# Delta-rule attention with a hard-swish MLP on one core: first steps reordered, runs of small matmuls joined in pairs

## The chip, the cores and the metric

The kernel runs on one core of a Trainium2 chip. The metric is the device time of one execution in microseconds (us), as the median of several. A profiled execution also gives a span, from its first to its last instruction, which is 2 us or so shorter. Ratios are the mean time of one kernel's runs over that of the kernel before in the same rounds on the same chip, so they are not quite the ratio of the medians that stand beside them. In the profile's lines PE is TensorE (PEld its weight loads), DVE is VectorE, ACT ScalarE, POOL GpSimd and SP SyncE; SPq and ACTq are the issuing of DMA transfers by SyncE and ScalarE.

## The reference

```python
# attention: q, k, v of (4, 8, 768, 48), beta of (4, 8, 768)
k_n = k / (np.linalg.norm(k, axis=-1, keepdims=True) + 1e-06)
for t in range(S):
    y[:, :, t] = np.einsum('bhd,bhde->bhe', q[:, :, t], state)
    v_old = np.einsum('bhde,bhd->bhe', state, kt)
    state = state + bt[:, :, :, None] * np.einsum('bhd,bhe->bhde', kt, vt - v_old)
# bridge to x of (3072, 384), then the MLP with w_in (384, 2048), w_out (2048, 384)
h = x @ w_in
g = h * np.clip(h + 3.0, 0.0, 6.0) / 6.0
out = g @ w_out
```

The weights arrive as 64-bit floats, so the kernel has to make 32-bit floats of them on the chip.

## The kernel before

The sequence is cut into 24 steps of 32 tokens, four steps to a group. What has to be told apart in the traces:

- **Norms** of a group's keys (a square, a reduction, a Newton iteration on VectorE).
- **Preparation** of one step: normalized keys kb and masks mb on GpSimd, eight transposes (pt) on TensorE, 64 small score matmuls (sc), the masked scores LB on VectorE, half of which go to DRAM.
- **Substitution** for a group: it reads the scores back as A, then does 30 pairs of VectorE operations (pr, A), and writes the result through DRAM into LB.
- **Chain** of one step: ks (state times keys), R = v - ks, pz (LB times R), Z, py (state times queries plus LB times Z), y, its transposes (yt, the "seam"), su (the state's update). Each of ks, pz, su, sc and the two halves of py is a run of 64 matmuls on 32x32 to 64x64 pieces of the array.
- **MLP units**: `up` makes one 128-column block of h (ph, 6 matmuls), ScalarE's t and VectorE's gate g; `down` is four matmuls into po.
- **Conversion** of one weight tile: five VectorE operations and one on ScalarE. Eight tiles make w_in, eight w_out; `need(n)` places conversions until n tiles are done.

The instructions of each engine stand in the order in which this Python text emits them, so the schedule is the order of the `take` calls:

```python
    def take(gen, n=1):                # emit the next n parts of a generator
        for _ in range(n):
            next(gen, None)
    ...
        for t in range(GS):            # GS = 4; queries, keys and weights all on SyncE
            load_k(GS + t)
        drain(norms(0, 0, 1))
    ...
        take(conv, 2)
        drain(norms(1, 0, GS))         # second norms, then the first substitution
        inv = inverse(0, nc.scalar)
    ...
        for t in range(CB):            # CB = 2
            load_v(t + 2)
            for _ in chain(t):
                take(conv, 2)          # two conversion operations per part of a chain
    ...
        for t in range(CB, N):         # the main loop: one step of the chain, 16 MLP units
            g, i = divmod(t, GS)
            load_v(t + 2)
            ...
            elif i == 2 and t + GS // 2 < N:
                fill = inverse(g + 1, nc.sync)
                for n in range(GS):
                    load_k((g + 2) * GS + n)
            ...
            for u in range(NU // 2 if early else NU):     # early: steps 2 and 3, 8 units each
                if i < 2 and preps:
                    at(u, preps[2 * i : 2 * i + 2])
                if early or u % 2 == 0:
                    take(ch)
                if early:
                    need(min(NWI, ((t - CB) * NU // 2 + u) // 2 + 1))
                else:
                    take(conv, 2)
                take(units)
                take(fill, 3 if early else 1 + (u % 2 == 0))
```

## Time and profile before

| | before |
|---|---|
| median of the first three runs | 855.86 us (854.84 to 857.21) |
| span of the profiled run | 853.4 us |
| busy: TensorE / VectorE / ScalarE / GpSimd | 82% / 40% / 22% / 9% |
| start of step 2, 4, 6 | 129.4, 193.6, 274.6 us |

The strip of the page cuts the span in 40 slices; a digit is the busy share of TensorE in tenths, and the second line is its granted clock. Before:

```profile
PE   1113248557789979999989999799999999999997
PEclk9966558687899979999989999999999999999999
```

TensorE is full from about the thirteenth slice on (one slice is 21.3 us), with a dip in the fifteenth, the twenty-first and the twenty-sixth; in front of that it is half empty, at a clock that falls to half. How the rest of the profile is read is the first part of the prediction.

### The profile page before, as it was taken

To read this page: it belongs to the slowest core of one execution; us is meant where nothing else is said; L and a number is where in the kernel's file an instruction comes from. 1 tells how busy PE (TensorE), PEld (TensorE's weight loads), DVE (VectorE), ACT (ScalarE), POOL (GpSimd) and SP (SyncE) were. 2 spreads that over 40 slices of the span, in tenths; PEclk is the share of its full clock that TensorE was granted. 3 is DMA by queue.
4 is the path that set the end of the run, shared out by engine and by line. 5 is a ranking of instruction groups with operands and counts; after the bars stand their busy time and mean duration, and the time that the engine had idled before them with its cause. 6 is when DMAs were issued, how large, how long until landed. Compare 5 with 4: busy or idle time off the path is not lost.

```text
span 853.4 us, 24929 instructions
## 1 busy us (share of the span) xinstructions
PE 703.6 (82%) x11208; PEld 507.6 (59%) x11208; DVE 344.5 (40%) x865; ACT 188.5 (22%) x377; POOL 78.8 (9%) x118
## 2 busy tenths in 40 slices
PE   1113248557789979999989999799999999999997
PEld 1112236444557657677567686586776867768684
DVE  5049663865562285022662122850237411212020
ACT  2121122122222014132132141141321312213030
POOL 3213300030210002100002200021000000000000
PEclk9966558687899979999989999999999999999999
DMA  5451573032421402122220214020120300000000
GB/s 114 100 118 29 132 205 73 2 96 77 128 64 41 91 20 60 29 50 49 66 56 19 44 28 95 20 61 18 27 49 19 72 12 20 2 20 2 19 0 19
DMA packets 140138, 45.76 MB, mean 54 GB/s; under 512 B 130272, under 2 KB 133344, under 8 KB 140032
## 3 DMA queue, kind: packets, MB, share of 16 engines
q1 hardware_dynamic: 127200, 41.45, 21.5%
q10 hardware_dynamic: 12832, 2.72, 1.6%
q8 instruction: 88, 1.44, 0.7%
q14 instruction: 18, 0.15, 0.1%
HBM read 33.13 MB, written 11.01 MB: 52 GB/s over the span
## 4 chain that ended last, share of the span: by engine, by line
PE 66%; DVE 11%; issue 8%; DMA 6%; SPq 5%; ACT 2%; POOL 1%; ACTq 0%; POOLq 0%; DVEq 0%
PE ph L469 29%; PE po L490 24%; SPq L86 4%; DVE pr L327 2%; DVE A L331 2%; DMA d<-in_moe_w_out_dram 2%; PE py L379 2%; PE pt L282 2%; PE pz L379 2%; PE su L438 2%; PE sc L295 2%; PE py L369 2%; PE ks L369 1%; DMA A<-l_dram 1%; DMA l_dram<-LB 1%
## 5 line engine op out<-in xcount | busy, mean ns | idle before, releaser
L469 PE MATMUL ph<-xT,w_in 128*128 128x256 f32 x1152 | 289.6, 403 | 17.5 <-DVE w_in L200 9.1
L490 PE MATMUL po<-w_out,g 128*128 128x384 f32 x768 | 272.2, 500 | 4.4 <-DVE w_out L200 4.4
L469 PEld LDWEIGHTS ph<-xT,w_in 128*128 128x128 f32 x1152 | 221.4, 199 | 54.1 <-DVE w_in L200 9.5
L490 PEld LDWEIGHTS po<-w_out,g 128*128 128x128 f32 x768 | 141.6, 193 | 89.3 <-DVE w_out L200 4.5
L478 DVE SCALAR_TENSOR_TENSOR g<-t,ph 128x256 f32<-128x256 f32 x192 | 80.5, 419 | 206.9 <-ACT t L474 206.9
L474 ACT ACTIVATE t<-ph,half 128x256 f32<-128x256 f32 x192 | 90.7, 473 | 224.4 <-PE ph L469 211.7
L327 DVE TENSOR_TENSOR pr<-A 128x30 f32<-128x30 f32 (+9 forms) x180 | 61.6, 342 | 65.8 <-DMA A<-l_dram 61.0
L282 PE MATMUL pt<-ident,kb 128*128 128x128 f32 x96 | 17.6, 314 | 57.7 <-POOL kb L260 57.7
L331 DVE TENSOR_TENSOR A<-A,pr 128x30 f32<-128x30 f32 (+9 forms) x180 | 61.3, 341 | 6.2
L260 POOL TENSOR_TENSOR kb<-kf,inv 128x384 f32<-128x384 f32 x24 | 21.2, 883 | 417.1 <-DVE inv L247 350.3
L282 PEld LDWEIGHTS pt<-ident,kb 128*128 128x128 f32 x96 | 13.1, 160 | 62.0 <-POOL kb L260 58.7
L285 ACT ACTIVATE KQ<-pt 128x512 f32<-128x512 f32 x48 | 28.2, 596 | 82.4 <-PE pt L282 54.4
L446 DVE TENSOR_TENSOR state<-state,su 128x384 f32<-128x384 f32 x46 | 23.3, 548 | 55.8 <-PE su L438 55.8
L301 DVE TENSOR_TENSOR LB<-sc,mb 128x512 f32<-128x512 f32 x24 | 16.4, 685 | 69.2 <-PE sc L295 69.2
L267 POOL TENSOR_TENSOR mb<-beta_tok,mask 128x256 f32<-128x256 f32 x48 | 34.3, 734 | 107.1 <-DVE LB L301 107.1
L496 ACT ACTIVATE o<-po 128x384 f32<-128x384 f32 x24 | 11.8, 492 | 141.7 <-PE po L490 141.7
L295 PE MATMUL sc<-KQ 64*32 64x64 f32 x1536 | 21.9, 242 | 20.8 <-ACT KQ L285 20.8
L379 PE MATMUL pz<-R,LB 32*32 32x48 f32 x1472 | 22.9, 216 | 19.3 <-issue 10.7
L379 PEld LDWEIGHTS pz<-R,LB 32*32 32x32 f32 x1472 | 19.7, 115 | 30.6 <-issue 19.0
L295 PEld LDWEIGHTS sc<-KQ 64*32 64x32 f32 x1536 | 17.9, 114 | 29.6 <-ACT KQ L285 22.9
L168 ACT ACTIVATE e<-e,rebias 128x768 uint32<-128x768 uint32 x16 | 15.0, 935 | 78.8 <-DVE e L165 71.8
L379 PEld LDWEIGHTS py<-Z,LB 32*32 32x32 f32 x1536 | 19.1, 109 | 20.5 <-issue 11.3
(54 smaller groups left out, 384.1 us busy)
## 6 DMA issues: line engine op xcount, KB each, us to landing
d<-in_moe_w_in_dram SPq DMA_DIRECT2D x8, 768.0 KB, 5.3
d<-in_moe_w_out_dram SPq DMA_DIRECT2D x8, 768.0 KB, 4.4
kf<-in_k_dram SPq DMA_DIRECT2D x96, 48.0 KB, 2.2
qb<-in_q_dram SPq DMA_DIRECT2D x96, 48.0 KB, 2.2
vf<-in_v_dram SPq DMA_DIRECT2D x96, 48.0 KB, 2.6
out_dram<-o SPq DMA_DIRECT2D x96, 48.0 KB, 1.6
A<-l_dram SPq DMA_DIRECT2D x5, 512.0 KB, 3.8
x_dram<-A SPq DMA_DIRECT2D x5, 512.0 KB, 3.1
```

Source lines behind the costliest of these rows:

```text
L86: nc.sync.dma_start(out=kfs[g][rows(b), i], in_=tokens(k, b, t))
L267: nc.gpsimd.tensor_tensor(out=mb[:, e], in0=beta_tok[:, t, e:H:2].unsqueeze(2).unsqueeze(3).to_broadcast([P, NP, 2, C]), in1=mask2[:].unsq ...
L282: nc.tensor.transpose(pt[:, p, :], src[:, 2 * p : 2 * p + 2].rearrange("p e w -> p (e w)"), ident[:])
L285: nc.scalar.activation(out=KQ[:, :, j, :], in_=pt[:], func=ACTF.Copy)
L295: nc.tensor.matmul(scv[rows(b), e, p], lhsT=KQ[r, p, 0, rows(b)], rhs=KQ[r, p, :, rows(b)], start=True, stop=True,)
L327: nc.vector.tensor_tensor(out=pv, in0=A[:, j, j + 1 :].unsqueeze(1).to_broadcast([128, j, n]), in1=A[:, 0:j, j].unsqueeze(2).to_broadcast( ...
L331: nc.vector.tensor_tensor(out=A[:, 0:j, j + 1 :], in0=A[:, 0:j, j + 1 :], in1=pv, op=ALU.subtract)
L379: nc.tensor.matmul(place(h, b), lhsT=m(h)[rows(b)], rhs=z[rows(b), D * h : D * h + D], start=start, stop=True, skip_group_check=True, tile ...
L469: nc.tensor.matmul(ph[:], lhsT=w_in[:, s, f * 128 : (f + 1) * 128], rhs=xT[:, s, :], start=(s == 0), stop=(s == NKT - 1),)
L474: nc.scalar.activation(out=t1[:], in_=ph[:], func=ACTF.Relu, bias=half[:, 0:1], scale=1.0 / 6.0)
L478: nc.vector.scalar_tensor_tensor(out=g[:], in0=t1[:], scalar=1.0, in1=ph[:], op0=ALU.min, op1=ALU.mult)
L490: nc.tensor.matmul(po[:], lhsT=gs[blk, f][:, c * P : (c + 1) * P], rhs=w_out[:, f, :], start=(f == 0), stop=(f == NFC - 1),)
```

## The change

The intent: start the MLP sooner, keep the waits of the first 275 us short, and make fewer and longer runs of small matmuls. Core of the diff (cuts marked with dots, the comments added here):

```diff
-    def load_q(t):
+    def load_q(t, eng=nc.sync):
...
     def convert():
-        split_w(0)                 # e of tile i+1 was made before tile i was finished
-        yield
         for i in range(NW):
-            split_w(i + 1)
-            yield
             if i in raws:          # now one tile from its first to its last operation
...
-                load_w(i + 2)      # in the middle of a conversion
...
             done[0] = i + 1
+            if i + 2 not in raws and i + 2 > 4:
+                load_w(i + 2)      # at its end
...
-            nc.scalar.activation(out=sq[:], in_=kf[:, i0 + i], func=ACTF.Square)
+            if g == 0:
+                nc.scalar.activation(out=sq[:], in_=kf[:, i0 + i], func=ACTF.Square)
+            else:
+                nc.gpsimd.tensor_tensor(
+                    out=sq[:], in0=kf[:, i0 + i], in1=kf[:, i0 + i], op=ALU.mult
+                )
...
             R = Rt[:]
+            of_state(py, 1)        # the state half of py directly behind ks
             yield
...
+        with tc.tile_pool(name="early", bufs=3) as early:    # raw tiles of weights 0 to 2
+            for t in range(GS):
+                load_k(t)
+                load_q(t, nc.scalar)
...
+            inv1 = norms(1, 0, GS)                           # second norms between the
+            for t in range(1, GS):                           # first preparations
...
+            need(1)
+            inv = inverse(0, nc.scalar)
+            take(inv)
+            for t in range(GS):                              # preparations 4 to 7 inside
+                take(prep_of(GS + t))                        # the first substitution
+                take(inv, 4)
...
+            need(2)
             for t in range(CB):
                 load_v(t + 2)
                 for _ in chain(t):
-                    take(conv, 2)
+                    take(conv)
+            for n in range(GS):
+                load_k(2 * GS + n)
+            need(3)
...
+            if i == 1 and (g + 2) * GS < N:                  # keys one step earlier
+                for n in range(GS):
+                    load_k((g + 2) * GS + n)
+            if i == 2 and t > CB:
+                drain(fill)
+                fill = chained(norms(g + 2, 0, GS) ..., inverse(g + 1, nc.sync) ...)
...
+            plan = {
+                0: lambda: (take(ch), now and take(now[1])),
+                3: lambda: (take(ch), now and take(now[0])),  # pz, then scores
+                7: lambda: (take(ch), now and take(now[1])),  # py, then scores
...
                 if early:
-                    need(min(NWI, ((t - CB) * NU // 2 + u) // 2 + 1))
+                    need(min(NWI, ((t - CB) * NU + u) // 4 + 1))
```

## The prediction

> **What bounds the kernel now.** I read the granted clock first (0.920 over the span, one core), then the strip of 40 slices, then busy times by stage, then timelines of the stages that lose time. I cut stages where a step's first run of small matmuls starts (ks, the state times the keys): step 2, the first with MLP work, at 129.7 us, step 4 at 193.6, step 6 at 274.6. The busy times by stage (columns: stretch, its length, then busy us and count of PE, PEld, DVE, ACT and POOL, the TensorE clock, the DMA share, GB/s):
>
> ```profile
> 0.00:129.70 129.70, 35.43 (x1102) 29.00 (x1102) 71.81 (x174) 23.89 (x39) 28.31 (x54) 0.72 0.50 115
> 129.70:193.57 63.87, 41.52 (x743) 31.13 (x735) 39.58 (x108) 12.72 (x27) 7.76 (x8) 0.77 0.25 57
> 193.57:274.58 81.01, 66.97 (x1096) 46.11 (x1095) 42.87 (x65) 21.44 (x39) 9.46 (x8) 0.91 0.30 79
> 274.58:853.40 578.82, 559.63 (x8279) 401.33 (x8278) 190.27 (x520) 130.43 (x273) 33.32 (x48) 0.98 0.17 36
> ```
>
> From step 6 on TensorE is the bound (560 of 579 us). Before it TensorE idles for 94, 22 and 14 us of the three stages: chains through DVE, DMA issue and ACT set the pace. The largest hole of the first stage, in the timeline:
>
> ```profile
> 22.75 7.85 SPq L86 DMA_DIRECT2D kf<-in_k_dram  x16
> 30.71 1.86 SPq L91 DMA_DIRECT2D qb<-in_q_dram  x4
> 32.68 0.39 SPq L157 DMA_DIRECT2D d<-in_moe_w_in_dram  x1
> 33.16 15.83 SPq L91 DMA_DIRECT2D qb<-in_q_dram  x12
> ...
> 38.04 0.56 DVE L165 TENSOR_SCALAR e<-d 128x768 uint32<-128x768 uint32 x1 [17.09 <-DMA d<-in_moe_w_in_dram]
> ```
>
> DVE stands 17.09 us for the second weight tile, because its issue is behind 16 key loads on SyncE; the scores of steps 1 to 3 are behind it in DVE's order. Later DVE does the second norms up to 64.7 us and only then the first substitution (30 pairs pr/A, 64.7 to 90.3).
>
> The late part has three stalls, in steps 7, 11 and 15. The last one, DVE and SyncE of steps 14 and 15:
>
> ```profile
> 517.19 8.33 SPq L86 DMA_DIRECT2D kf<-in_k_dram  x16
> 525.56 0.45 SPq L318 DMA_DIRECT2D A<-l_dram  x1
> 530.34 0.19 DVE L327 TENSOR_TENSOR pr<-A 128x30 f32<-128x30 f32 x1 [13.60 <-DMA A<-l_dram]
> ...
> 541.11 1.00 PE L369 MATMUL ks<-state,KQ 64*32 64x48 f32 x64
> ...
> 548.73 0.55 DVE L394 TENSOR_TENSOR R<-vf,ks 128x384 f32<-128x384 f32 x1
> ...
> 549.38 1.50 PE L379 MATMUL pz<-R,LB 32*32 32x48 f32 x64 [4.48 <-issue]
> ```
>
> The substitution's input A was issued behind 16 key loads (8.33 us), so DVE started it late; ks ended at 541.9 but R, behind the backlog in DVE's order, ran at 548.7, and pz waited 4 us ("issue" hides that DVE was the cause). Step 15 took 541.11 to 573.36, 32.25 us, against 25.87 for the like step 18 (632.62 to 658.49): 6.4 lost. Step 7 took 32.58 (6.7 lost) and step 11 33.75 (7.9 lost); step 6, at 29.36, ended with 3.4 idle of the same kind, step 10 with 0.6. Together 25 us.
>
> **What the Trainium skill says.** Four places.
> "DMA: Bandwidth & Descriptors", section "Issuing engines are not separate DMA queues": transfers of all issuers run on the same 16 engines, and several issuers save only issue time. The trace agrees that issue time matters: 12 query loads held SyncE for 11.36 us early and 15.83 us later. At 0.50 DMA share in the first stage the engines themselves have room.
> "TensorEngine Tiling (Array Packing)", section "Key Properties": changing the tiling mode drains TensorE. The trace agrees that a run of small matmuls costs more than its matmuls: below.
> "TensorE: Matmul & The Clock Gate", Part 1: the clock is halved until TensorE has been busy. The trace agrees: the 64-matmul pz run took 1.50 us at 549.4, after the stall, and 0.88 at 636.1.
> "SBUF — State Buffer", section "SBUF: two separate sides": DVE with two SBUF inputs and GpSimd lock each other out. The trace agrees: pr of 128x58 took 0.73 us beside GpSimd's kb (65.1) and 0.22 alone (530.8).
>
> **The change part by part.**
> *Queries on ACT's queue, more weights early.* SyncE issues 8 x 4 key loads at 0.49 us each (5.88/12), then the first weight tile, done by about 18 us; the others follow without being in front of anything. The hole of 22 to 38 us goes. The price: ACT's first Square stands behind 16 query issues at about 0.45 us, so the first norms start near 13 instead of 6, and the first three steps' norms end near 26.7 instead of 19.5 (+7).
> *Second norms ahead, squares on GpSimd.* From 27 us GpSimd does three preparations of about 3.0 us (kb 0.83, mb 1.2 to 1.5, bkb 0.83) and four squares of 0.85 us, each waiting for a DVE reduce of 0.55 as the buffer is single. My chain has the last scores (LB of step 3) on DVE at 46.5; before it was 49.3. The second norms, 57 to 64.7 before, are by then done. One weight conversion (4.2 us: 0.5+0.5+0.9+0.9+0.9 plus gaps, from the rows at 240 us) follows; A lands near 52, so the substitution starts at 52.5 instead of 64.7 (-12).
> *First substitution and first two chains.* It took 25.6 us; two score products (0.7 each) and half a microsecond of conversion are now inside it: 52.5 to about 80. Before, 90.3 to 129.7 (39 us) held the remaining preparations, six conversions and two chains, with score writes on ACT's queue (ACT waited 7.02 us behind one). Now the preparations are mostly inside the substitution and their writes on SyncE; left are the way out and back through DRAM (about 6 us), chain 0 (Z to the next ks: 4.6 us before, plus 2), chain 1 (about 9 without its 3 us stall), so step 2 starts at about 102 (-28).
> *Steps 2 and 3.* DVE work: norms paced by GpSimd 9, substitution 23.5, 4.2 conversions 18, gates g 16 x 0.35 = 6, R and state 3, together 60 us, in one in-order queue with the matmuls' evacuation. So DVE bounds this stage: 61 us, about what it was (63.9). Step 4 at 163.
> *Steps 4 and 5.* In before a w_out tile came each 7.5 us (conversions at 202, 209.5, 219.6, 228.9, 235): splitting tile i+1 makes DVE wait for its load before tile i frees its buffer. The new order finishes one tile before touching the next, and two loads overlap: (4.2 + 4.4 load)/2, some 4.5 us a tile. Step 4 becomes about 37 us (DVE-bound: 7.4 tiles x 4.2 + g, R, state), step 5 30: 67 instead of 81. Step 6 at 230; I add 3 for waits I have not seen: 233 (-42).
> *From step 6 on.* Key loads come a step earlier and the substitution behind the norms, its A load then near the step's start; DVE starts it about 9 us into the step, instead of 15 to 19, and 16 of 30 pairs fit before the next R. I count all 25 us as gone.
> *Joins.* A ks run has matmuls of 0.20 us in 0.80 us for 64, so (0.80-0.20)/63 = 9.5 ns each, 0.61 us; it costs 3.51 us from ks (632.62) to pz (636.13) less 8 x 0.3226 for the po between, 0.93 us. So entering and leaving costs about 0.3. Joining ks with the state part of py (same shape, 18 times from step 6) saves 0.3 each, 5.4; pz or py with scores (different shapes, 12 times) perhaps 0.2, 2.4. Sum 7.8.
> So the last stage: 578.8-25-7.8 = 546. Span 233+546 = 779; the run's time is 2.5 above the span (855.86 to 853.4): 782.
>
> **The rivals.**
> *Joins cost instead of save.* Z and the gates come in longer unbroken gaps, and py holds one of two PSUM buffers from the start of the step, so the second scores could wait for y's copy (0.5 us plus ACT's queue). Speaks for it: only two buffers. Against: TensorE then has MLP work before and after, and ks's buffer is free again. Worth 8 lost plus up to 8 more: about 795.
> *The stalls move rather than go.* Norms ahead push the substitution's end 8 takes later, so LB of the next group could be late at pz of steps 8, 12, 16. I get A done near 19 us into the step and 6 us for DRAM, against pz at about 30: some 4 to 5 us of room. If wrong, 3 x 4 us back: about 794.
> *The start is only shifted.* ACT's late start (+7), GpSimd's longer work beside the substitution's two-input operations, and a DVE-bound steps 2 and 3 could eat the gain of the first stage: steps 2 to 6 at +12, about 794; all of this together, 815.
> *Better than that.* If steps 4 and 5 are TensorE-bound already (29.6 us each, as step 16), 8 less, and with a start as computed: about 770.
>
> **Range and chances.** Each large term has an independent support: 16 us hole and 25 us stalls are seen directly, 14 us in steps 4 and 5 follow from a seen cycle. Even half of all (74 us) is 4%. Time 782 us; 8 in 10 between 764 and 804. Faster by over 2%: 0.97; within 2%: 0.02; slower: 0.01.
>
> **What will show it.** Right: no DVE wait over 5 us for a weight tile in the first 50 us; the first pr before 55 us; step 2 near 102, step 4 near 163, step 6 near 233; steps 7, 11, 15 within 1 us of step 18; ks and py as one run of 128 in about 1.4 us; step 18 some 0.3 us shorter. Wrong: R of steps 7, 11, 15 still late, pz of steps 8, 12, 16 waiting for LB, a joined pair longer than 1.9 us, or DVE idle in steps 2 and 3 (then a wait, not DVE's work, bounds them).

## The result, and the profile after

| | before | after |
|---|---|---|
| median | 855.35 us (853.76 to 857.21, 4 runs) | 807.32 us (803.47 to 808.87, 4 runs) |
| ratio | | 0.9429, interval 0.9397 to 0.9462 |
| span of the profiled run | 853.4 us | 801.8 us |
| granted clock | 0.920 | 0.945 |

The kernel became 5.7% faster, well clear of noise, but 25 us slower than the 782 us predicted and 3 us outside of the range of 764 to 804. The strip after:

```profile
PE   0351483457879999999999999999999999999997
PEclk9996586578999999999999999999999999999999
```

The dips in the full part are gone, and the full part begins with the thirteenth slice, which is now 20.0 us long. The busy times by stage answer to the first fence of the prediction (columns: stretch, length, busy us and count of PE, PEld, DVE, ACT, POOL, clock, DMA share, GB/s); the cuts are again the starts of steps 2, 4 and 6:

```profile
0.00:104.55 104.55, 36.41 (x1095) 29.69 (x1095) 59.41 (x157) 18.38 (x30) 31.80 (x58) 0.81 0.52 111
104.55:186.57 82.02, 44.48 (x752) 34.59 (x751) 53.19 (x123) 15.08 (x28) 9.65 (x13) 0.72 0.30 82
186.57:256.44 69.87, 59.81 (x1088) 43.06 (x1087) 43.44 (x66) 21.61 (x39) 9.10 (x8) 0.98 0.44 109
256.44:801.80 545.36, 541.00 (x8279) 395.39 (x8278) 200.27 (x520) 126.80 (x261) 42.60 (x59) 1.00 0.17 36
```

Set against the sum of the prediction (which cut step 2 of the kernel before at 129.7 instead of 129.4):

| stage | before | predicted | measured | off by |
|---|---|---|---|---|
| up to step 2 | 129.4 | 102 | 104.55 | +2.6 |
| steps 2 and 3 | 64.1 | 61 | 82.02 | **+21.0** |
| steps 4 and 5 | 81.0 | 67 | 69.87 | +2.9 |
| set aside for waits not seen | | 3 | | -3 |
| step 6 to the end | 578.8 | 546 | 545.36 | -0.6 |
| span | 853.4 | 779 | 801.8 | +22.8 |

So one stage holds nearly the whole miss, and it became 18 us longer than before although everything around it became shorter. In it VectorE is busy for 53.2 us, TensorE for 44.5 us, of 82.0: neither is full. The profiled execution is the fastest of its series, so the stages account for 22.8 of the 25 us; the rest is mostly scatter between executions.

**The stalls of the late part are gone.** Two groups tell it (columns: line, engine, operation, output and inputs, shapes, count, then busy us and mean ns, then the idle time before them and what ended most of it). Before:

```profile
L327 DVE TENSOR_TENSOR pr<-A 128x30 f32<-128x30 f32 (+9 forms) x180 | 61.6, 342 | 65.8 <-DMA A<-l_dram 61.0
L469 PE MATMUL ph<-xT,w_in 128*128 128x256 f32 x1152 | 289.6, 403 | 17.5 <-DVE w_in L200 9.1
```

After:

```profile
L320 DVE TENSOR_TENSOR pr<-A 128x30 f32<-128x30 f32 (+9 forms) x180 | 66.8, 371 | 5.9 <-DMA A<-l_dram 1.7
L460 PE MATMUL ph<-xT,w_in 128*128 128x256 f32 x1152 | 278.8, 395 | 43.4 <-DVE w_in L188 36.9
```

VectorE waited 61 us in all for the substitution's input, now 1.7. Steps 7, 11 and 15 take 26.47 us each, where they took 32.58, 33.75 and 32.25. The second line of each pair shows what came instead: the ph matmuls, which before waited 9.1 us for converted w_in tiles, now wait 36.9.

**The wait that took their place.** Where those 36.9 us lie, in the timeline of step 3 after (start, length, engine, line, operation, count, and in brackets the idle time before and its releaser). One turn of the wheel, from one conversion's last operation to the next one's:

```profile
143.88 0.96 DVE L188 SCALAR_TENSOR_TENSOR w_in<-m,e 128x768 f32<-128x768 f32 x1
144.89 5.49 PE L460 MATMUL ph<-xT,w_in 128*128 128x256 f32 x12 [6.66 <-DVE w_in L188]
147.91 0.48 ACT L465 ACTIVATE t<-ph,half 128x256 f32<-128x256 f32 x1 [5.43 <-PE ph L460]
148.42 0.42 DVE L469 SCALAR_TENSOR_TENSOR g<-t,ph 128x256 f32<-128x256 f32 x1 [3.59 <-ACT t L465]
148.76 0.40 DVE L320 TENSOR_TENSOR pr<-A 128x240 f32<-128x240 f32 x1
...
154.01 0.55 DVE L168 TENSOR_SCALAR e<-d 128x768 uint32<-128x768 uint32 x1
...
156.93 0.96 DVE L188 SCALAR_TENSOR_TENSOR w_in<-m,e 128x768 f32<-128x768 f32 x1
157.94 5.49 PE L460 MATMUL ph<-xT,w_in 128*128 128x256 f32 x12 [6.69 <-DVE w_in L188]
```

VectorE finishes a tile at 144.8. TensorE has stood for 6.66 us for just this tile and starts. VectorE's next entry is the gate of these very matmuls, so now VectorE stands, for 3.59 us, until the first six of them and ScalarE's t are through. Then it does substitution pairs and the next tile (148.8 to 157.9), and TensorE, done with its matmuls at 151.3, stands again. For most of the turn one works while the other waits. The turn takes 13.05 us of VectorE's time: 3.6 of standing, 0.3 for the gate, 5.2 of pairs (with the tile's second gate), 3.9 of conversion. Four tiles go this way in step 3 (the later turns, with fewer or shorter pairs, take 12.2 and 11.1 us), which takes 49.7 us with VectorE busy for 32.1.

Step 2 has another form of it. The matmuls of the fourth tile waited 12.93 us, up to 131.4, for one operation of 0.95 us that the schedule had left to stand behind nine substitution pairs (the expectation below says ten) and the state's update:

```profile
129.50 1.01 DVE L437 TENSOR_TENSOR state<-state,su 128x384 f32<-128x384 f32 x2
130.42 0.95 DVE L188 SCALAR_TENSOR_TENSOR w_in<-m,e 128x768 f32<-128x768 f32 x1
131.43 5.49 PE L460 MATMUL ph<-xT,w_in 128*128 128x256 f32 x12 [12.93 <-DVE w_in L188]
```

**The start.** The hole of 17 us is gone, and the price for the second queue is there. ScalarE issues queries from 3.87 to 13.46 us, and only then comes to the first Square:

```profile
3.87 9.59 ACTq L90 DMA_DIRECT2D qb<-in_q_dram  x15
13.62 1.28 ACT L209 ACT_TABLE_LOAD   x1 [13.62 <-DMA kf<-in_k_dram]
14.92 0.52 ACT L209 ACTIVATE sq<-kf 128x384 f32<-128x384 f32 x1
...
55.53 0.19 DVE L320 TENSOR_TENSOR pr<-A 128x30 f32<-128x30 f32 x1 [1.72 <-DMA A<-l_dram]
```

The releaser in the second line is misleading: it names the keys, whose first issue by SyncE was at 0.81 us; in the experiment below with only three queries left in that place the same instruction ran at 5.77 us. What ended at 13.46 is the issuing. The first substitution starts at 55.5 us, against 64.7 before.

### The profile page after: what moved, and what is told of

Its sections match the earlier page's. It is cut to its first block, busy times and chain, and to the rows that moved or that the text cites. A ratio compares the mean times of both kernels' runs of the same rounds, so it can differ in the third digit from the quotient of the medians.

```text
span 801.8 us, 24917 instructions
## 1 busy us (share of the span) xinstructions
PE 681.7 (85%) x11208; PEld 502.7 (63%) x11208; DVE 356.3 (44%) x865; ACT 181.9 (23%) x357; POOL 93.1 (12%) x138
## 4 chain that ended last, share of the span: by engine, by line
PE 76%; DVE 13%; DMA 4%; SPq 2%; issue 2%; POOL 1%; ACT 1%; ACTq 0%; POOLq 0%; DVEq 0%
PE po L481 31%; PE ph L460 31%; DVE A L324 3%; DVE pr L320 3%; PE pz L372 2%; PE py L372 2%; PE su L429 2%; PE pt L275 2%; PE ks L362 2%; SPq L85 2%; PE sc L288 2%; PE py L362 1%; DMA qb<-in_q_dram 1%; DVE m L179 1%; DVE e L183 1%
## 5 line engine op out<-in xcount | busy, mean ns | idle before, releaser
L460 PE MATMUL ph<-xT,w_in 128*128 128x256 f32 x1152 | 278.8, 395 | 43.4 <-DVE w_in L188 36.9
L481 PE MATMUL po<-w_out,g 128*128 128x384 f32 x768 | 265.1, 494 | 4.1 <-DVE w_out L188 4.1
L324 DVE TENSOR_TENSOR A<-A,pr 128x30 f32<-128x30 f32 (+9 forms) x180 | 67.9, 377 | 6.2
L320 DVE TENSOR_TENSOR pr<-A 128x30 f32<-128x30 f32 (+9 forms) x180 | 66.8, 371 | 5.9 <-DMA A<-l_dram 1.7
L278 ACT ACTIVATE KQ<-pt 128x512 f32<-128x512 f32 x48 | 28.2, 597 | 87.4 <-PE pt L275 74.2
L211 POOL TENSOR_TENSOR sq<-kf 128x384 f32<-128x384 f32 x20 | 17.0, 852 | 175.9 <-DMA kf<-in_k_dram 109.4
L288 PE MATMUL sc<-KQ 64*32 64x64 f32 x1536 | 22.8, 249 | 12.7 <-ACT KQ L278 12.6
L214 DVE TENSOR_REDUCE ss<-sq 128x8 f32<-128x384 f32 x24 | 13.3, 552 | 38.4 <-POOL sq L211 24.2
L388 DVE TENSOR_TENSOR R<-vf,ks 128x384 f32<-128x384 f32 x23 | 12.7, 551 | 37.1 <-PE ks L362 37.1
```

Of the source, the lines that this page charges most:

```text
L278: nc.scalar.activation(out=KQ[:, :, j, :], in_=pt[:], func=ACTF.Copy)
L288: nc.tensor.matmul(scv[rows(b), e, p], lhsT=KQ[r, p, 0, rows(b)], rhs=KQ[r, p, :, rows(b)], start=True, stop=True,)
L320: nc.vector.tensor_tensor(out=pv, in0=A[:, j, j + 1 :].unsqueeze(1).to_broadcast([128, j, n]), in1=A[:, 0:j, j].unsqueeze(2).to_broadcast( ...
L324: nc.vector.tensor_tensor(out=A[:, 0:j, j + 1 :], in0=A[:, 0:j, j + 1 :], in1=pv, op=ALU.subtract)
L460: nc.tensor.matmul(ph[:], lhsT=w_in[:, s, f * 128 : (f + 1) * 128], rhs=xT[:, s, :], start=(s == 0), stop=(s == NKT - 1),)
L481: nc.tensor.matmul(po[:], lhsT=gs[blk, f][:, c * P : (c + 1) * P], rhs=w_out[:, f, :], start=(f == 0), stop=(f == NFC - 1),)
```

## The experiments

Theory A, for the 21 us: the conversions of w_in stand directly in front of the matmuls that need them, and the gates of those matmuls directly behind, so VectorE and TensorE hand over in turns. Theory B is the prediction's own: VectorE's amount of work in steps 2 and 3 is the bound, and I only counted it too low (the 53.2 us busy, under the 60 predicted, already speak against this). Theory C: the raw tiles come late from DRAM. For the rest of the change there were smaller questions: what the joins are worth, what took the stalls away, and whether the second queue's price is on the path.

### The yardstick

The changed kernel again, five rounds, so that the runs beside it have a value from their own chip. Three sections below (keys one step earlier, the substitution ahead, only the first queries) and the first candidate ran on another chip; they are compared with it by their ratios too.

> The changed kernel unedited, as the yardstick for the runs beside it. All theories: 803 to 809 us, steps 2 and 3 together 82 us, from step 6 to the end 545 us.

Measured: 805.78 us (803.74 to 808.32), ratio 0.9421. From step 6 to the end 545.3 us, as in the first profile; steps 2 and 3 took 85.5 us in this profile, 82.0 in the other. So 3.5 of the 4.8 us between these two executions lie in that stage, and a few us between variants mean little there.

### w_in conversions one tile earlier

```diff
-                    need(min(NWI, ((t - CB) * NU + u) // 4 + 1))
+                    need(min(NWI, ((t - CB) * NU + u) // 4 + 2))
```

> The changed kernel, but in steps 2 and 3 each conversion of a w_in tile is placed one tile (two MLP units) earlier in the order. Theory A (hand-over: matmuls wait for the tile converted just before them, and DVE then waits for their gate g, in turns): steps 2 and 3 shrink from 82 to about 60 us, the wait of the ph matmuls for w_in (36.9 us) falls below 15, time about 20 us lower, 787. Theory B (my prediction's: DVE's amount of work in these two steps is the bound): the same work stays, 82 us within 3, time 804 to 810. Theory C (weight tiles land late): no change either, with DVE waiting for tile loads before the conversions.

Measured: 787.10 us (785.14 to 791.17), ratio 0.9204; 18.7 us below the yardstick by the medians. Steps 2 and 3 take 65.3 us (26.67 and 38.65). The stage, with the same number of VectorE instructions (123) as in the changed kernel:

```profile
104.08:169.40 65.32, 44.28 (x752) 34.55 (x751) 52.41 (x123) 13.88 (x28) 10.33 (x13) 0.77 0.35 98
```

And its turn of the wheel, step 3:

```profile
131.08 0.55 DVE L168 TENSOR_SCALAR e<-d 128x768 uint32<-128x768 uint32 x1
...
132.51 0.82 ACT L465 ACTIVATE t<-ph,half 128x256 f32<-128x256 f32 x2
...
134.00 0.96 DVE L188 SCALAR_TENSOR_TENSOR w_in<-m,e 128x768 f32<-128x768 f32 x1
134.88 0.41 DVE L469 SCALAR_TENSOR_TENSOR g<-t,ph 128x256 f32<-128x256 f32 x1
...
135.21 0.37 DVE L320 TENSOR_TENSOR pr<-A 128x210 f32<-128x210 f32 x1
```

ScalarE's t was done at 133.3, while VectorE was still converting the next tile, so the gate at 134.88 has no bracket: VectorE did not stand. In steps 2 and 3 VectorE's wait for t fell from 19.9 to 2.8 us (15 gates in each), the matmuls' wait for w_in from 36.9 to 18.7. The work (52.4 us busy) is what it was; the stage lost 17 to 20 us. Theory A's time was met to a tenth of a microsecond, which is luck: its 60 us for the stage was missed (65.3), and so was its bound of 15 us for the wait on w_in (18.7); VectorE is still the busier of the two, and TensorE still waits for it. Theory B alone is out, since the amount of work did not change. Theory C is out by the trace of the changed kernel itself: in steps 2 and 3 the first operations of the conversions (e<-d) waited 0.0 us for their raw tiles.

### The fourth tile finished before step 2

```diff
-            need(3)
+            need(4)
```

> The changed kernel, but the fourth w_in tile is finished before step 2 starts, where now its last operation stands in step 2 behind ten substitution pairs and the state update. Theory A: the 12.9 us wait of the matmuls in step 2 goes, step 2 shrinks from 32.3 to about 22, step 3 keeps its 50: time 8 to 11 us lower. Theory B: one operation of 1 us is only moved, time within 2 us.

Measured: 801.42 us (798.92 to 803.50), ratio 0.9355: 4.4 us below the yardstick, half of what I expected. Step 2 fell to 28.2 us, not to 22; step 3 took 52.7 (49.7 and 51.8 in the two profiles of the changed kernel). The 12.93 us wait did go, but the next ks then waited 9.32 us for the state's update, which stood behind the same substitution pairs:

```profile
132.23 1.35 PE L362 MATMUL ks<-state,KQ 64*32 64x48 f32 x61 [9.32 <-DVE state L437]
```

Moving one operation of an engine that is behind removed little of the wait here: the next of its results was waited for instead (9.32 of the 12.93 us).

### All w_in tiles before the MLP starts

```diff
-            need(3)
+            need(8)
```

> The changed kernel, but all eight w_in tiles are converted before step 2, as in the kernel before, where five conversions now stand in steps 2 and 3. Theory A (hand-over): step 2 starts 18 to 22 us later (five times 4.2 and loads), but steps 2 and 3 fall from 82 to 40 to 48, so step 4 starts near 168, time about 788. Theory B (DVE's amount of work): what leaves steps 2 and 3 is paid before them, step 4 at 186 within 3, time 803 to 810.

Measured: 788.71 us (787.47 to 789.86), ratio 0.9201. The time and step 4's start (170.8) are theory A's; the split is not as I wrote it, and "as in the kernel before" in the expectation is not exact: that kernel had six tiles before its step 2. The ks run of step 2 does not need the converted tiles and started at 105.9, about as ever (104.6 and 105.5), so the conversions came to lie inside step 2 (44.8 us), and step 3 took 20.1. Together 64.9 us:

```profile
105.90:170.82 64.92, 36.05 (x751) 29.01 (x750) 53.51 (x122) 14.89 (x28) 9.64 (x13) 0.78 0.32 88
```

Same VectorE work, done first and without hand-over: 64.9 us. With one tile of lead: 65.3. Just in time: 82.0 to 85.5. So theory B has its part too, as the floor: once the hand-over is loose, some 53 us of VectorE work and about 12 us of waits (with all tiles first, 6.4 of them for raw tiles) set this stage, not far from the 61 predicted.

### Joined runs taken apart

```diff
+            if t >= CB:
+                yield
             of_state(py, 1)
...
-                3: lambda: (take(ch), now and take(now[0])),
+                1: lambda: take(ch),
+                3: lambda: take(ch),
+                4: lambda: now and take(now[0]),
...
-                7: lambda: (take(ch), now and take(now[1])),
+                7: lambda: take(ch),
+                8: lambda: now and take(now[1]),
```

> The changed kernel with the joined runs of small matmuls taken apart again: the state part of py one MLP unit after ks, the scores one unit after pz and after py, all else as it is. Prediction: 0.3 us for each of 18 pairs and 0.2 for each of 12 from step 6 on, 7.8 us slower, step 18 at 25.87 again. Rival, joins do nothing (the shorter steps come from the moved order): within 2 us. Rival, joins cost (waits for a PSUM buffer): 3 us or more faster.

Measured: 816.29 us (815.32 to 819.50), ratio 0.9546, so 10.5 us slower. Step 18 took 25.86 us, as in the kernel before, against 25.51 joined: 0.35 for a pair of the same shape. Steps with two preparations took 28.80 instead of 28.05: 0.75 for one such pair and two pairs with scores, so 0.20 each for the latter. From step 6 on that makes 18 x 0.35 + 12 x 0.20 = 8.7 us, and the stage is indeed 8.8 longer (817.8 - 263.7 against 806.6 - 261.3). Steps 4 and 5 became longer too (73.9 against 70.3 us), which was not followed up. The timeline of step 16 joined, a pz run followed by scores:

```profile
532.00 0.88 PE L372 MATMUL pz<-R,LB 32*32 32x48 f32 x64
532.81 0.86 PE L288 MATMUL sc<-KQ 64*32 64x64 f32 x64
533.60 2.85 PE L481 MATMUL po<-w_out,g 128*128 128x384 f32 x8
```

and apart:

```profile
544.76 0.88 PE L372 MATMUL pz<-R,LB 32*32 32x48 f32 x64
545.57 1.56 PE L483 MATMUL po<-w_out,g 128*128 128x384 f32 x4
547.06 0.86 PE L288 MATMUL sc<-KQ 64*32 64x64 f32 x64
547.85 1.56 PE L483 MATMUL po<-w_out,g 128*128 128x384 f32 x4
```

Each small run occupies the same time either way. What is saved is one change to the large matmuls and back: start of pz to the end of the eighth po is 4.45 us joined and 4.65 apart. The rivals (joins do nothing, joins cost a wait for a buffer in PSUM, where the matmuls' results lie) are out.

### The kernel before, with keys one step earlier from step 9 on

```diff
+            elif i == 1 and g >= 2:
+                for n in range(GS):
+                    load_k((g + 2) * GS + n)
             elif i == 2 and t + GS // 2 < N:
                 fill = inverse(g + 1, nc.sync)
-                for n in range(GS):
+                for n in range(GS if g < 2 else 0):
                     load_k((g + 2) * GS + n)
```

> The kernel before, with one edit: from step 9 on the 16 key loads are issued one step earlier, so that they no longer stand in front of the substitution's input A on SyncE. Theory Q (the stalls of steps 11 and 15 come from this queue order alone): steps 11 and 15 fall from 33.75 and 32.25 to about 25.9, step 7 keeps its 32.6, time 14 to 15 us below before, about 840. Rival (the stalls went because the norms now stand ahead of the substitution): no change, 855.

Measured: 840.38 us (838.22 to 843.23), ratio 0.9828, interval 0.9793 to 0.9862: faster clear of noise, though not clearly by 2%. Steps 11 and 15 fell from 33.75 and 32.25 to 25.95 us; step 7, left alone on purpose, kept 32.59. The input A now follows the value loads directly:

```profile
398.34 2.11 SPq L97 DMA_DIRECT2D vf<-in_v_dram  x4
...
400.55 0.40 SPq L318 DMA_DIRECT2D A<-l_dram  x1
...
404.58 0.19 DVE L327 TENSOR_TENSOR pr<-A 128x30 f32<-128x30 f32 x1 [4.58 <-DMA A<-l_dram]
```

The first pair starts 6.1 us into step 10 (which began at 398.5), where in step 14 of the kernel before it started 15.1 us in. Where the key loads stand on SyncE makes or unmakes the stalls of steps 11 and 15. That step 7 is of the same kind was not tested in this kernel.

### The substitution ahead of the norms again

```diff
                 fill = chained(
-                    norms(g + 2, 0, GS) if (g + 2) * GS < N else iter(()),
                     inverse(g + 1, nc.sync) if (g + 1) * GS < N else iter(()),
+                    norms(g + 2, 0, GS) if (g + 2) * GS < N else iter(()),
                 )
```

> The changed kernel, with the substitution ahead of the next norms again, as before; the key loads stay a step early. Theory Q: no stalls come back, steps 7, 11, 15 within 1.5 us of 26.5, time 803 to 810. Rival (order of norms): steps 7, 11 and 15 at 32 again, time about 823.

Measured: 805.03 us (803.17 to 806.61), ratio 0.9412: as the yardstick. Steps 7, 11 and 15 stay at 26.47 us. So in the changed kernel the order of norms and substitution has no part in it.

### Only the first queries on the second queue

```diff
             for t in range(GS):
                 load_k(t)
-                load_q(t, nc.scalar)
+            load_q(0, nc.scalar)
+            for t in range(1, GS):
+                load_q(t)
             for t in range(GS):
                 load_k(GS + t)
```

> The changed kernel, with only the first step's queries on ACT's queue; those of steps 1 to 3 on SyncE behind the first 16 key loads. Theory D (the price of the second queue is on the path: ACT's first Square waits behind 16 query issues, 14.9 us against 6.0 before): the first norms start at 6 to 7 us, step 2 at about 97 instead of 104.5, time 6 to 9 us lower. Rival (GpSimd's preparations and squares or the loads set the pace from there on): step 2 within 2 us of 104.5, time within 3.

Measured: 799.82 us (798.71 to 803.41), ratio 0.9359: 6 us below the yardstick by the medians, 5 by the ratios. The first Square runs at 7.06 us and step 2 starts at 96.6:

```profile
3.79 1.81 ACTq L90 DMA_DIRECT2D qb<-in_q_dram  x3
5.77 1.28 ACT L209 ACT_TABLE_LOAD   x1 [5.77 <-DMA kf<-in_k_dram]
7.06 0.52 ACT L209 ACTIVATE sq<-kf 128x384 f32<-128x384 f32 x1
```

So the price of the second queue was on the path: all of the 7.9 us between the two first Squares arrive at step 2. Not all are kept: step 2 took 36.4 us instead of 32.3 (VectorE waited 9.4 us for GpSimd's squares there, 5.2 before), and step 4 starts 4.0 us earlier than in the first profile of the changed kernel.

### Candidates to beat both

First, conversions two tiles ahead (`// 4 + 3`), the queries as above, and the third group of keys issued before the first two chains instead of after them:

> A candidate to beat both: the changed kernel with w_in conversions placed two tiles earlier in steps 2 and 3, only the first queries on ACT's queue, and the third group of keys issued before the first two chains instead of after. If the terms add: 19 from the hand-over, 3 more from the second tile, 7 from the queries, 4 from the keys (waits of GpSimd's squares for keys in step 2): 806 less 33, about 773. Theory B (DVE's amount of work) leaves little of it: steps 2 and 3 not under 78.

Measured: 786.63 us (784.14 to 787.59), ratio 0.9201, not 773. Moving the keys did not help: on SyncE they now stand in front of the values, and R of step 2 waited for these instead of GpSimd's squares for the keys. Steps 2 and 3 took 64.2 us, so theory B's 78 is out here too.

```profile
109.01 0.56 DVE L388 TENSOR_TENSOR R<-vf,ks 128x384 f32<-128x384 f32 x1 [6.24 <-DMA vf<-in_v_dram]
```

Then without that move of the keys, with one and with two tiles of lead:

> The two edits that helped together: w_in conversions one tile earlier in steps 2 and 3, only the first queries on ACT's queue; keys where the change has them. If the two gains add (19 and 6): 781 us, step 4 at about 163.

> The same with conversions two tiles earlier. The candidate before this lost 6 us in step 2 to value loads that stood behind the moved keys; without that move, and if the second tile frees what DVE still waited (some 13 us idle in steps 2 and 3 with one tile): steps 2 and 3 at 58 to 62 us, time 776 to 780. Rival (one tile of lead is all that the hand-over needs, DVE's work bounds the rest): equal to the run with one tile within 2 us.

Measured: one tile 784.52 us (780.77 to 786.80), ratio 0.9145, interval 0.9110 to 0.9180; two tiles 781.91 us (780.04 to 783.16), ratio 0.9117, interval 0.9092 to 0.9142. Steps 2 and 3 take 66.2 and 63.9 us, so the second tile did not bring the 58 to 62 that I expected, and the two are the same within their intervals. Both times missed what was expected by a few us (781, and 776 to 780). With two tiles the ph matmuls of steps 2 and 3 no longer waited for w_in at all, and the stage kept its length with VectorE busy for 52.5 us: the rival in the expectation, that one tile is enough for the hand-over and VectorE's work bounds the rest, fits best. Both beat both kernels: two tiles of lead, with the queries of steps 1 to 3 put back on SyncE, make 0.9117 of the kernel before and 0.967 (0.9117 / 0.9429) of the changed one.

## Why the prediction was wrong

**The step that failed** is the one headed "Steps 2 and 3", in its words: "DVE work: ... together 60 us, in one in-order queue with the matmuls' evacuation. So DVE bounds this stage: 61 us, about what it was (63.9)." The work was not counted too low (53.2 us busy). What failed is the conclusion that a stage with one busiest engine takes that engine's work. It does so only if the engine never stands. Here the schedule let two engines wait for one another in turns: a conversion directly in front of its matmuls, their gate directly behind. I had read both facts in the diff, the call `need` placed at each unit and the gate inside the unit, and had even written "in one in-order queue", but I added up durations instead of walking once around the loop. The first fence of the prediction held a warning that I passed over: in the same two steps of the kernel before, VectorE was busy for only 39.6 of 63.9 us, so waits set that stage already. One walk, with the durations of this trace, gives 3.9 + 2.9 + 0.5 + 0.4 + 5.2 = 12.9 us a tile (conversion, six matmuls at the halved clock, t, gate, pairs) against 13.05 measured. The term was 61 and measured 82.0 (85.5 in a second profile). One tile of lead makes it 65.3, all tiles in front 64.9, with the same work: this is shown. How much of the 3.6 us of standing comes from the half clock is only argued: six ph matmuls took 2.9 us there (granted clock 0.50 from 144.9 to 147.8 us) and 1.56 at full clock (1.00 at 113.6 us), so some 1.3 of it.

The kernel before did not have this loop because it had converted six of the eight w_in tiles before step 2, two operations per chain part. The change halved that (`take(conv)` for `take(conv, 2)`), which moved the conversions to where they have to be handed over; how much it did for the earlier start of step 2 was not measured by itself.

**The start** was right within 2.6 us: 102 against 104.55. By its parts: the first Square at 14.9 us where I had the norms near 13; the first pair at 55.5 against 52.5; the substitution's end at 81.5 against 80; chain 1 took 11.0 us where I had about 9. The price of the second queue, +7 in the prediction, was +8.9 at the first Square (14.92 against 6.02), and it could have been avoided.

**Steps 4 and 5** were 69.9 against 67. I had said some 4.5 us a w_out tile; from the first conversion (187.88) to the eighth (229.91) it is 42.03 / 7 = 6.0. Step 4 was longer than said (41.9 against 37), step 5 shorter (28.0 against 30). I had called step 4 DVE-bound; in the two steps VectorE was busy for 43.4 and TensorE for 59.8 of 69.9 us, and the po matmuls waited only 4.1 us for converted tiles. What holds the tiles up there was not tested and stays open. That the sum came near is partly luck: the errors of the two steps have opposite signs, and the 3 us that I had set aside covered what was left.

**From step 6 on** the prediction was right to 0.6 us: the 25 us of stalls went, by the cause given (keys in front of A on SyncE, shown for steps 11 and 15 by moving nothing else), and the joins gave 0.35 and 0.20 us where 0.3 and 0.2 were said. The signs named for this part came as written: steps 7, 11 and 15 within 0.96 us of step 18, ks with its py half in about 1.4 us (583.07 to 584.45 in step 18).

**The rivals.** "Joins cost" and "the stalls move" did not come. "The start is only shifted" named steps 2 to 6 at +12 and a DVE-bound stage as its cause; the size was nearer to what came than my main line, but the cause was not. The right sign stood last in the list of what would prove me wrong: VectorE idle in steps 2 and 3, "then a wait, not DVE's work, bounds them". It was idle for 28.8 of 82.0 us. My range was too narrow because I took the terms as independent and gave this stage, the only one built on a sum of work instead of on a seen wait, no more room than the others.

**Small slips in the working**, which change little: ks of step 15 ended at 542.1 us (541.11 + 1.00), not 541.9; the five conversions listed for w_out start 8.2 us apart in the mean, not 7.5; and the 2.5 us from span to time set a median against the span of one execution, which itself took 855.14 us for its 853.4.

## What to carry to other kernels

When two in-order engines feed each other, walk once around the loop in the emitted order, with every handover, before taking the busier one's work for the stage's time; if producer and consumer stand next to each other in the order, give the producer one item of lead. A load that is not urgent must not be issued in front of one that is, on the same queue: 16 such loads cost 6 to 8 us per group here, and a group of keys moved ahead of the values made a new wait of 6 us in one of the candidates. Small runs of matmuls between large ones are worth joining, a few tenths of a microsecond a pair.

## What the Trainium skill lacked or had wrong

- "TensorEngine Tiling (Array Packing)", section "Key Properties", says that a change of tiling mode drains TensorE, but not what that costs. Here joining two runs of 64 small matmuls saved 0.35 us if both had the same mode (64x32) and 0.20 us if they had two different small modes (32x32 and 64x32), each time between full-array matmuls.
- "DMA: Bandwidth & Descriptors", section "Issuing engines are not separate DMA queues", calls the issue time usually small relative to the transfer. For these 48 KB loads it was not: one issue took about a quarter of the time to landing (15 query issues held ScalarE for 9.59 us, 0.64 each, against a median of 2.3 us from issue to landing of the query loads on SyncE), and issues of one engine add up: the queries delayed ScalarE's first Square from 6.0 to 14.9 us, and 16 key issues held SyncE for 7.9 to 10.6 us.
- None of the four pages that the prediction drew on says that two in-order engines which hand over in turns can both be far from full: here 82.0 us with VectorE busy for 53.2 and TensorE for 44.5, and 65.3 us with the same work (52.4 and 44.3 us) and one tile of lead.
